# The second DFT stage and its inverse as 64x64 products on quarters of the array, with the exchanged rows from a second product

## The chip, the cores and the metric

The kernel runs on one core of a Trainium2 chip. A core has TensorE (PE, matrix products, with its weight loads listed as PEld), VectorE (DVE), ScalarE (ACT), GpSimd (POOL) and SyncE (SP, which here only issues transfers). Products go from SBUF to PSUM, which DVE and ACT empty. The metric is device time in microseconds, median of several runs; lower is better.

## The reference, cut to what matters

```python
def _A_ref(q, k, v, shift_k, ssm_k, ssm_D):      # B, S, D = 1, 2048, 640
    ...                                          # k_shift: 4-tap causal convolution of k
    kv = k_shift * v
    kv_f = rfft2(pad(kv, 2 * S), axes=(1, 2))    # per channel, length 4096
    kf_f = rfft2(pad(ssm_k, 2 * S))
    y = irfft2(kv_f * kf_f)[:, 0, :S, :] + kv * ssm_D
    return q * y

x = A_q
xn = layernorm(x)
s = _A_ref(xn, A_k, A_v, A_shift_k, A_ssm_k, A_ssm_D)
g = silu(gelu(xn @ w1 + b1) @ w2 + b2)           # F = 1728
return x + s * g
```

So there is a long convolution of kv with a filter for every channel, done by way of the frequency domain, and beside it a two-layer feed-forward network (FFN) over the same rows, whose output gates the convolution's.

## The kernel before, in words

**The convolution** is a DFT in two stages, written as matrix products in bf16. The filter and kv each go through the first stage (steps kf and uf, whole 128x128 weights WA and WB), are cast from PSUM to SBUF (ke, ue), stored to DRAM (ks, us: scrK, scrU) and loaded back in another order of rows (fl: kin; ml: uin). The second stage works on 32 groups g of 128 rows and 640 channels. Its weight matrix `mats[:, 0]` (F2m) holds four 32x32 blocks on the diagonal and zeros elsewhere; each block maps the rows of one small transform, with cosine and sine parts in alternating rows.

- `ff g` (k_f2, line 479): the filter's second stage, one call of mm2 (line 335), which makes two products, one for each half of 320 channels, into one "big" PSUM tile. `fe g` casts it into `Khat[:, g, :]`, on ACT or DVE.
- `mk g2` (swap_load, line 515): two copies by DMA on SP's queue, which put the rows of two groups of Khat into a ring buffer with each even row exchanged with the odd row beside it. The ring is the last 8 of Khat's 40 rows.
- `mu g` (u_f2, line 520): the second stage of kv, mm2 with the same weights, into one big tile.
- `mp g` (product, line 523): one DVE instruction of 1280 elements a partition. It multiplies the tile of mu with Khat and with the exchanged Khat, and so gives all four partial products of a complex multiplication as a pair tile p.
- `mc g` (inv1, line 530): the inverse of the second stage, for each half two accumulating products, with weights I1a on p's first part and I1b on its second, into one big tile. `me g` (line 537) casts it to SBUF on ACT or DVE, and `ms g2` (line 540) stores two groups to scrC on POOL's queue.

After that, `yl` loads scrC back, `y` makes the last inverse stage (whole weights GA, GB), and `yt`, `yo`, `ys` gate, add and store.

**The FFN** runs in four chunks of 512 rows. `h` (ffn1, line 373) is five products of 512 columns, `he` the GELU on ACT; `g` (ffn2, line 391) is 14 products of 320 columns, `ge` the SiLU on ACT and `gm` a multiplication on DVE. `tt` and `it` are transposes on PE, `te` and `ie` empty them.

**The order of all work is written by hand**: PLAN, lines 30 to 71, is a list of steps, and each engine works through its instructions in that order. Every engine's queue, that of PE too, is in order. Semaphores follow from tiles: an instruction that first writes a buffer waits for the last reader of the tile that held it before.

**PSUM** has 8 banks. `ps_ffn` has two tiles of one bank (h, g, tt). `ps_big` (line 108) has three tiles of two banks; ff, uf, kf, mu, mc, it, kt and y take them in turn, each from its first product to the cast or product that reads it. In the stage looked at here, PLAN runs for example `mu5 mp5 mk6 h31 he31 ml6 ff20 fe20.a mc3 me3.a ms1 ln15 mu6 mp6 mc4 me4.a mu7 mp7`: FFN steps fill PE between the convolution's.

Of the kernel before, what the change touches and what calls it, by code (L numbers as in the profile page):

```python
# [30 lines left out]
em K0 sp s A0 h0 h1 P2 ee.a A1 P1 P0 pt pb he0 he1 h2 he2 h3 he3 h4 he4 h5 he5 h6 he6 h7 he7 h8 he8 h9 he9 h10
he10 h11 he11 h12 he12 h13 he13 K3 ss cv8 cv0 B w cv1 cv2 cv3 cv4 cv5 cv6 cv9 cv10 cv11 cv12 cv13 cv14 K1 cv16
X1 ls4 ls5 ls7 ls6 lv1 C0 X3 cv17 cv18 g0 ge0 gm0 g1 ge1 gm1 ws0 cv19 g2 ge2 g3 ge3 g4 cv20 cv21 cv22 ws1 g5 lr1
ln7 ln5 ws2 C4 C3 C1 V0 cv7 cv15 C2 d kt0 kc0.a kt1 kc1.a kf0 kf1 ke0.a kt2 kc2.a V1 ln4 kf2 ke2.a cv24 cv23 X2
cv25 ke1.d ks0 gm2 ge4 ln6 kf3 ke3.d ks1 kf4 ke4.a gm4 ge5 kt3 kc3.d kf5 ke5.a ks2 V2 tt7 te7.a kt5 kc5.d tt9
te9.a kt4 gm5 kf7 cv26 cv27 cv28 kf6 kc4.a ke6.a ke7.a ks3 g6 ge6 kf8 ke8.a kf9 ke9.d ks4 kf10 ke10.a K2 tt8
te8.a kt6 kc6.d kf11 ke11.a ks5 kt9 kc9.d gm3 kf12 ke12.a tt5 te5.d tt6 te6.a uf1 kt7 kf13 kc7.a ke13.a ks6 g7
ge7 ls12 uf0 ue0.a ue1.d us0 cv29 cv30 cv31 V3 h14 he14 kf14 ke14.d kf15 ke15.d ks7 h15 he15 kt8 kc8.d kf19 kf18
ke18.a ke19.d ks9 kt10 kc10.a cv32 cv33 cv34 cv35 cv36 kf16 ke16.a kt12 cv40 kf17 kc12.a ke17.a ks8 h16 he16 uf3
uf2 ue2.a ue3.a us1 h17 he17 kf21 kf20 ke20.a ke21.d ks10 kt11 kc11.a h18 he18 uf5 uf4 ue4.a ue5.d us2 kf22  # L40
ke22.d ls10 h19 he19 kt14 kf24 ke24.d sm kf23 kc14.a ke23.a ks11 h20 he20 kf25 ke25.d ks12 kt13 kc13.d kf28
ke28.a h21 he21 uf6 ue6.a kf29 ke29.a ks14 uf7 ue7.a us3 h22 he22 h23 he23 kf26 ke26.a gm7 cv37 cv38 cv41 cv42
cv39 kf27 ke27.a ks13 kt15 kc15.d kf30 ke30.a kf31 ke31.a ks15 fl0 fl1 fl2 h24 he24 fl4 uf10 ue10.a gm6 ls15 ls8
ls9 uf8 ue8.a ls14 uf11 ue11.a us5 h25 he25 h26 he26 uf14 ue14.a cv43 ls13 lv3 lr3 h27 he27 cv44 ls11 lv2 lr2
cv45 cv46 cv47 uf12 ue12.a uf9 ue9.a us4 fl3 uf15 ue15.a us7 g8 ge8 gm8 ln13 ln9 uf13 ue13.a us6 fl5 g9 ge9 ff3
fe3.a ln12 ff1 fe1.d ln10 ff2 fe2.a cv56 ff0 fe0.a cv48 cv49 cv50 ln8 uf21 uf20 ue20.a ue21.a us10 ff8 fe8.a
ln11 g10 ge10 uf16 ue16.a ff6 fe6.d gm9 ff9 fe9.a fl7 ff5 fe5.a ff7 fe7.a fl9 ff4 fe4.a fl8 uf17 ue17.a us8 g11
ge11 cv51 cv52 cv53 cv54 cv55 ff11 fe11.a ff10 fe10.a fl6 uf18 ue18.d uf19 ue19.a us9 fl11 uf26 ue26.a cv57 cv58
cv59 uf24 ue24.a uf27 ue27.a us13 uf25 ue25.a us12 fl12 ff16 fe16.d ff17 fe17.a fl15 ff12 fe12.a tt12 te12.a
ff14 fe14.a cv60 cv61 cv62 cv63 ff18 fe18.a ff15 fe15.a fl13 g12 ff19 fe19.a fl10 uf22 ue22.d ff13 fe13.a fl14  # L50
uf31 gm11 ge12 uf30 ue30.a ue31.d us15 ff23 fe23.d gm12 uf23 ue23.a us11 gm10 tt14 te14.d uf29 uf28 ue28.d
ue29.a us14 mk0 ml0 ml1 mk1 mk2 mk3 ml2 ml3 ml5 ml4 ff31 fe31.a tt13 te13.a tt10 te10.d it0 ie0.d ff27 fe27.d
ff25 fe25.d g13 ge13 gm13 g14 ge14 gm14 ff29 fe29.d ln14 ff28 fe28.a ff24 fe24.d g15 ge15 gm15 ff21 fe21.a tt11
te11.d ff22 fe22.a mu0 mp0 ff26 fe26.a ml7 h28 he28 mu2 mp2 ml10 ml8 mu1 mp1 mk4 mc0 me0.a h29 he29 ff30 fe30.a
mu3 mp3 mk5 ml12 h30 he30 ml11 mc2 me2.a mu4 mp4 mc1 me1.a ms0 mu5 mp5 mk6 h31 he31 ml6 ff20 fe20.a mc3 me3.a
ms1 ln15 mu6 mp6 mc4 me4.a mu7 mp7 mk7 ml9 h32 he32 mu8 mp8 mc5 me5.a ms2 mc6 me6.a mu11 mp11 mc7 me7.a ms3 mu10
mp10 h33 he33 mu9 mp9 mk8 mk9 mc8 me8.a mc10 me10.a mu12 mp12 mu13 mp13 mk10 mc11 me11.a ms5 ml14 h34 he34 ml15
mc12 me12.a it1 ie1.d mc13 me13.a ms6 mu15 mp15 h35 he35 mu14 mp14 mk11 ml13 mc9 me9.a ms4 mu18 mp18 h36 he36
mc14 me14.a mu17 mp17 h37 he37 mu16 mp16 mk12 mc15 me15.a mu20 mp20 h38 he38 mu19 mp19 mk13 mc18 me18.a h39 he39
mu21 mp21 mk14 mc16 me16.a tt17 mc19 me19.a ms9 mc17 me17.a ms8 mu23 mp23 mc20 me20.a mu22 mp22 mk15 h40 he40  # L60
mc21 me21.a ms10 mu24 mp24 mu25 mp25 mc22 me22.a h41 he41 te17.d mc24 me24.a mu26 mp26 mc25 me25.a ms12 tt15
te15.a mu27 mp27 tt16 te16.d mc23 me23.a ms11 mc26 me26.a tt18 te18.d mu29 mp29 it3 ie3.a mu28 mp28 g16 ge16
gm16 mc27 me27.a ms13 it2 ie2.d tt19 te19.a mu31 mp31 mu30 mp30 ms7 q0 g17 ge17 gm17 mc28 me28.a mc31 mc29
me29.d ms14 mc30 me30.d me31.d ms15 yl5 yl2 yl0 yl4 yl3 yl1 yl6 yl11 yl15 q1 g18 ge18 gm18 g19 ge19 gm19 g20
ge20 gm20 g21 ge21 gm21 g22 ge22 gm22 g23 ge23 gm23 h42 he42 h43 he43 y0 yt0 yo0 h44 he44 h45 he45 h46 he46 y5
yt5 yl8 y4 yt4 yo4 yo5 ys2 y1 yt1 yo1 ys0 y3 yt3 h47 he47 h48 he48 h49 he49 h50 he50 h51 he51 y2 yt2 yl7 yl14
yl9 yl10 yl12 yo2 yo3 ys1 q2 h52 he52 h53 he53 h54 he54 h55 he55 y6 yt6 yl13 yo6 y7 yt7 yo7 ys3 q3 y8 yt8 yo8
y11 yt11 g24 ge24 g25 ge25 g26 y12 yt12 gm24 ge26 gm25 ga24 ga25 gs25 y15 yt15 g27 ge27 y14 yt14 y13 yt13 gm26
ga26 gm27 ga27 gs27 y9 yt9 yo9 ys4 y10 yt10 yo10 yo11 ys5 g28 ge28 gm28 ga28 g29 ge29 gm29 ga29 g30 ge30 gm30
ga30 gs30 g31 ge31 gm31 ga31 gs29 gs31  # L70
"""


# [1 line left out]
def kernel(  # L75
# [170 lines left out]
    sm = {}  # L246
# [49 lines left out]
                             bias=sin_bias[:])  # L296

    def small_mats():
        nc.vector.tensor_tensor(out=mats[:], in0=sm["sn"], in1=sm["mask"], op=ALU.mult)
# [35 lines left out]
    def mm2(ps, lhsT, rhs, start=True, stop=True):  # L335
        for h in range(2):
            nc.tensor.matmul(out=ps[:, h, 0:HALF], lhsT=lhsT, rhs=rhs[:, h * HALF:(h + 1) * HALF], start=start, stop=stop)  # L337
# [174 lines left out]
    def uin_load(g2):  # L512
        nc.sync.dma_start(out=take(("uin", g2), pools["line"], None, None, None), in_=pair_view(scrU)[g2])

    def swap_load(g2):
        ks = take(("ks", g2), pools["ring"], None, None, "ks")
        for a in range(2):
            nc.sync.dma_start(out=ks[a:P:2, :, :], in_=Khat[1 - a:P:2, 2 * g2:2 * g2 + 2, :])
# [4 lines left out]
    def product(g):
        p = pair_of(("p", g))
        swap = NG + g % NR
        nc.vector.tensor_tensor(out=p[:].rearrange("p k (h c) -> p k h c", h=2),  # L526
                                in0=live["mu", g][:, None, :, 0:HALF].to_broadcast([P, 2, 2, HALF]),
                                in1=Khat[:, g:swap + 1:swap - g, :].rearrange("p k (h c) -> p k h c", h=2), op=ALU.mult)

    def inv1(g):  # L530
        p, psC = live["p", g], big_of(("mc", g))
        for h in range(2):
# [1 line left out]
            nc.tensor.matmul(out=psC[:, h, 0:HALF], lhsT=I1a, rhs=p[:, 0, hs], start=True, stop=False)  # L534
            nc.tensor.matmul(out=psC[:, h, 0:HALF], lhsT=I1b, rhs=p[:, 1, hs], start=False, stop=True)  # L535
# [171 lines left out]
```

## Time and profile before

| what | value |
|---|---|
| median of 3 runs | 229.04 us (227.22 to 229.06) |
| span of the profiled execution, first to last instruction | 225.2 us |
| PE busy | 209.3 us |
| DVE busy | 183.2 us |
| ACT busy | 149.7 us |
| DMA: 50.7% by the hardware queue, 20.6% by POOL's | share of 16 engines' span |

The page gives the span of the profiled execution and not what lies around it; the median of the runs is 3.84 us above this span. A row of the groups reads: line, engine, operation, out<-in, shape, count, then busy time in us, mean ns of one, then idle time of the engine just before and who ended it. Products are pipelined: one is listed with some 0.3 us, from its start to its modelled end, while the next starts well before that. A row of the timeline has the start in us from the span's start, the length, and "xN" where N instructions in a row were put together.

### The profile page before, as it was taken

The page shows a single profiled execution, that of the slowest core. Times are in us where ns is not written, and L with a number is a line of the kernel's source. Part 1 is how long each engine was busy: PE and PEld are TensorE (multiplying, and loading weights), DVE is VectorE, ACT ScalarE, POOL GpSimd, SP SyncE. Part 2 cuts the span into 40 slices and gives each one's busy share as a digit, 9 for nine tenths or more (in the row PEclk, how much of TensorE's full clock was granted, in tenths as well). Part 3 has the DMA queues.
Part 4 walks back from the last instruction along what each step waited for, and adds up shares of the span by engine and source line. Part 5 has one row for each costly group of instructions (what it writes and reads, how often), then busy time and mean ns, then how long its engine had stood idle before and what let it go on. Part 6 is the DMA issues. An engine that isn't in the chain of part 4 may idle for free.

```text
span 225.2 us, 3912 instructions
## 1 busy us (share of the span) xinstructions
PE 209.3 (93%) x1420; PEld 131.5 (58%) x1420; DVE 183.2 (81%) x309; ACT 149.7 (66%) x232; POOL 42.5 (19%) x72
## 2 busy tenths in 40 slices
PE   7869989899999899979999988999999999999993
PEld 4624457677555556645765544565777755457771
DVE  7799999989989999999859998999996125445792
ACT  3946697998988999999549665576762263671111
POOL 8000011032232345030200221203222000100010
...
GB/s 215 347 381 357 406 410 277 218 193 198 303 186 189 178 209 388 185 320 324 320 167 286 335 399 361 273 231 254 273 118 140 215 367 153 119 260 388 80 92 116
DMA packets 25209, 57.61 MB, mean 256 GB/s; under 512 B 2854, under 2 KB 14055, under 8 KB 25190
## 3 DMA queue, kind: packets, MB, share of 16 engines
q1 hardware_dynamic: 20726, 39.66, 50.7%
q0 software_dynamic: 4320, 17.70, 20.6%
...
## 4 chain that ended last, share of the span: by engine, by line
PE 59%; issue 13%; ACT 11%; DVE 7%; DMA 7%; SPq 1%; POOL 1%; DVEq 0%; POOLq 0%; ACTq 0%
PE g L396 20%; PE h L377 20%; ACT Khat L135 5%; DMA prm<-in_B_b_dram 4%; PE uf L337 3%; PE mc L534 2%; DMA scrC<-c 2%; PE mc L535 2%; PE kf L337 2%; PE mu L337 2%; PE y L553 2%; PE y L554 2%; DVE p L526 2%; DVE Khat L136 2%; PE ff L337 1%
## 5 line engine op out<-in xcount | busy, mean ns | idle before, releaser
L377 PE MATMUL h<-xnT,w_sb 128*128 128x512 bf16 x280 | 65.8, 379 | 1.3 <-ACT hT L383 1.0
L396 PE MATMUL g<-w_sb,hT 128*128 128x320 bf16 x448 | 63.7, 299 | 0.6 <-ACT sl L401 0.6
L396 PEld LDWEIGHTS <-hT 128*128 128x128 bf16 x448 | 43.8, 98 | 18.1 <-issue 0.8
L383 ACT ACTIVATE hT<-h,b_f 128x512 bf16<-128x512 f32 (+1 forms) x56 | 38.3, 690 | 23.2 <-PE h L377 20.7
L526 DVE TENSOR_TENSOR p<-mu,Khat 128x1280 bf16<-128x1280 f32 x32 | 45.8, 1484 | 3.1 <-PE mu L337 2.1
L377 PEld LDWEIGHTS <-w_sb 128*128 128x128 bf16 x280 | 27.3, 98 | 29.3 <-issue 1.5
L401 ACT ACTIVATE sl<-g 128x320 bf16<-128x320 f32 x32 | 14.0, 439 | 36.1 <-PE g L396 32.5
L135 ACT CAST c<-mc 128x640 bf16<-128x640 f32 x29 | 19.9, 692 | 6.5 <-PE mc L535 5.7
L541 POOL DMA_DIRECT2D scrC<-c x16 | 11.5, 718 | 51.9 <-ACT c L135 47.7
L406 DVE TENSOR_TENSOR xn<-xn,sl 128x320 bf16<-128x320 bf16 x32 | 10.0, 320 | 13.7 <-ACT sl L401 13.5
L469 DVE TENSOR_TENSOR uc<-uc,kvtmp 128x1280 bf16<-128x1280 bf16 x24 | 19.8, 824 | 0.7
L473 DVE TENSOR_TENSOR kvtmp<-kh,w_exp 128x1280 bf16<-128x1280 bf16 x24 | 19.7, 819 | 0.5
L534 PE MATMUL mc<-p,mats 128*128 128x320 bf16 x64 | 18.1, 298 | 1.6 <-DVE p L526 1.1
L560 DVE TENSOR_TENSOR t<-y,xn 128x640 bf16<-128x640 f32 x12 | 9.8, 820 | 10.6 <-PE y L554 10.5
L337 PEld LDWEIGHTS <-mats 128*128 128x128 bf16 x128 | 12.0, 97 | 10.8 <-issue 3.8
L535 PE MATMUL mc<-p,mats 128*128 128x320 bf16 x64 | 18.1, 298 | 0.0
L135 ACT CAST Khat<-uf 128x640 bf16<-128x640 f32 x26 | 17.0, 697 | 0.4 <-PE uf L337 0.4
L135 ACT CAST Khat<-ff 128x640 bf16<-128x640 f32 x24 | 15.5, 699 | 0.5 <-PE ff L337 0.4
L135 ACT CAST Khat<-kf 128x640 bf16<-128x640 f32 x22 | 15.1, 711 | 0.3 <-PE kf L337 0.2
L437 POOL DMA_DIRECT2D scrK<-Khat x16 | 8.9, 554 | 29.7 <-ACT Khat L135 16.6
L337 PE MATMUL mu<-kh,mats 128*128 128x320 bf16 x64 | 13.6, 298 | 0.8 <-DMA kh<-scrU 0.4
L337 PE MATMUL ff<-kin,mats 128*128 128x320 bf16 x64 | 12.3, 298 | 1.3 <-ACT Khat L135 1.3
...
## 6 DMA issues: line engine op xcount, KB each, us to landing
...
```

The costliest lines, as they stand in the source:

```text
L135: return nc.scalar.copy(out=out_ap, in_=in_ap)
L337: nc.tensor.matmul(out=ps[:, h, 0:HALF], lhsT=lhsT, rhs=rhs[:, h * HALF:(h + 1) * HALF], start=start, stop=stop)
L377: nc.tensor.matmul(out=ps[:, :], lhsT=w1_sb[:, t, ft * P:(ft + 1) * P], rhs=xnT[:, t, :], start=(t == 0), stop=(t == DT - 1))
L383: nc.scalar.activation(out=hT[0:M, ft, :], in_=live["h", i][0:M, :], func=ACT.Gelu_apprx_tanh, bias=b1_f[0:M, ft:ft + 1], scale=1.0)
L396: nc.tensor.matmul(out=ps[:, 0:HALF], lhsT=hT[0:M, ft, q * P:(q + 1) * P], rhs=w2_sb[0:M, ft, hs], start=(ft == 0), stop=(ft == FT - 1))
L401: nc.scalar.activation(out=sl[:], in_=live["g", i][:, 0:HALF], func=ACT.Silu)
L469: nc.vector.tensor_tensor(out=uc[:], in0=uc[:], in1=kvtmp[:], op=ALU.add)
L473: nc.vector.tensor_tensor(out=(kvtmp if s else uc)[:], in0=kh[:, r0:r0 + KC, :], in1=w_exp[:, j:j + 1, :].to_broadcast([P, KC, D]), op=ALU ...
L526: nc.vector.tensor_tensor(out=p[:].rearrange("p k (h c) -> p k h c", h=2), in0=live["mu", g][:, None, :, 0:HALF].to_broadcast([P, 2, 2, HA ...
L534: nc.tensor.matmul(out=psC[:, h, 0:HALF], lhsT=I1a, rhs=p[:, 0, hs], start=True, stop=False)
L535: nc.tensor.matmul(out=psC[:, h, 0:HALF], lhsT=I1b, rhs=p[:, 1, hs], start=False, stop=True)
L541: nc.gpsimd.dma_start(out=pair_view(scrC)[g2], in_=live["c", g2][:])
```

## The change

It does four things and leaves the rest of the program as it is.

1. `ff`: each of the two products becomes two of 64x64 weights, from the two diagonal blocks of F2. For one half of the channels the blocks' outputs go to the same half of the partitions as the inputs, for the other half of the channels to the opposite one, so that the four products of a group use the four quarters of the array.
2. `mu`: the same, and a second set with F2X, a copy of F2 with neighbouring columns exchanged, which gives the result with exchanged rows. Each half of the channels gets a big PSUM tile of its own: bank 0 the plain result, bank 1 the exchanged one. A mu thus has eight products and two big tiles.
3. `mp`: one instruction for each half (mp 2g and mp 2g+1), which multiplies both banks of the half's tile with Khat. The step `mk` is gone, and with it its 32 copies.
4. `mc`: four quarter products for I1A and four for I1B, accumulated, which put the partitions back in order.

`small_mats` makes the matrix F2X with two DVE copies. In PLAN the 16 `mk` steps are left out and each `mp g` is replaced in place by `mp 2g, mp 2g+1`; nothing else in the order changes.

```diff
-    mats = consts.tile([P, 3, P], BF16, name="mats")
-    F2m, I1a, I1b = (mats[:, i, :] for i in range(3))
+    mats = consts.tile([P, 4, P], BF16, name="mats")
+    F2, I1A, I1B, F2X = range(4)
+    QB = 64
...
     def small_mats():
-        nc.vector.tensor_tensor(out=mats[:], in0=sm["sn"], in1=sm["mask"], op=ALU.mult)
+        nc.vector.tensor_tensor(out=mats[:, 0:3, :], in0=sm["sn"], in1=sm["mask"], op=ALU.mult)
+        for c in range(2):
+            nc.vector.tensor_copy(out=mats[:, F2X, c::2], in_=mats[:, F2, 1 - c::2])
...
+    def blocks(out, m, rhs, turn, start=True, stop=True):
+        for i in range(P // QB):
+            j = (i + turn) % (P // QB)
+            a, b = (slice(x * QB, (x + 1) * QB) for x in ((i, j) if m in (F2, F2X) else (j, i)))
+            nc.tensor.matmul(out=out[b, :], lhsT=mats[a, m, a], rhs=rhs[a, :], start=start, stop=stop)
+
+    def half(h):
+        return slice(h * HALF, (h + 1) * HALF)
...
     def k_f2(g):
-        mm2(big_of(("ff", g)), F2m, live["kin", g // 2][:, g % 2, :])
+        ps = big_of(("ff", g))
+        for h in range(2):
+            blocks(ps[:, h, 0:HALF], F2, live["kin", g // 2][:, g % 2, half(h)], 2 * g + h)
...
-    def swap_load(g2):
-        ks = take(("ks", g2), pools["ring"], None, None, "ks")
-        for a in range(2):
-            nc.sync.dma_start(out=ks[a:P:2, :, :], in_=Khat[1 - a:P:2, 2 * g2:2 * g2 + 2, :])
-
     def u_f2(g):
-        mm2(big_of(("mu", g)), F2m, live["uin", g // 2][:, g % 2, :])
-
-    def product(g):
+        ps = [big_of(("mu", 2 * g + h)) for h in range(2)]
+        for x, m in enumerate((F2, F2X)):
+            for h in range(2):
+                blocks(ps[h][:, x, 0:HALF], m, live["uin", g // 2][:, g % 2, half(h)], 2 * g + h)
+
+    def product(i):
+        g, h = divmod(i, 2)
         p = pair_of(("p", g))
-        swap = NG + g % NR
-        nc.vector.tensor_tensor(out=p[:].rearrange("p k (h c) -> p k h c", h=2),
-                                in0=live["mu", g][:, None, :, 0:HALF].to_broadcast([P, 2, 2, HALF]),
-                                in1=Khat[:, g:swap + 1:swap - g, :].rearrange("p k (h c) -> p k h c", h=2), op=ALU.mult)
+        nc.vector.tensor_tensor(out=p[:, :, half(h)], in0=live["mu", i][:, :, 0:HALF],
+                                in1=Khat[:, g:g + 1, half(h)].to_broadcast([P, 2, HALF]), op=ALU.mult)
 
     def inv1(g):
         p, psC = live["p", g], big_of(("mc", g))
-        for h in range(2):
-            hs = slice(h * HALF, (h + 1) * HALF)
-            nc.tensor.matmul(out=psC[:, h, 0:HALF], lhsT=I1a, rhs=p[:, 0, hs], start=True, stop=False)
-            nc.tensor.matmul(out=psC[:, h, 0:HALF], lhsT=I1b, rhs=p[:, 1, hs], start=False, stop=True)
+        for x, m in enumerate((I1A, I1B)):
+            for h in range(2):
+                blocks(psC[:, h, 0:HALF], m, p[:, x, half(h)], 2 * g + h, x == 0, x == 1)
```

More of the change, by code (lines that the diff above doesn't have):

```diff
@@ L30 @@
 PLAN = """
[L31 to L70, printed above, removed]
+em K0 sp s A0 h0 h1 P2 ee.a A1 P1 P0 pt pb he0 he1 h2 he2 h3 he3 h4 he4 h5 he5 h6 he6 h7 he7 h8 he8 h9 he9 h10 he10
@@ new lines @@
+h11 he11 h12 he12 h13 he13 K3 ss cv8 cv0 B w cv1 cv2 cv3 cv4 cv5 cv6 cv9 cv10 cv11 cv12 cv13 cv14 K1 cv16 X1 ls4 ls5
+ls7 ls6 lv1 C0 X3 cv17 cv18 g0 ge0 gm0 g1 ge1 gm1 ws0 cv19 g2 ge2 g3 ge3 g4 cv20 cv21 cv22 ws1 g5 lr1 ln7 ln5 ws2 C4
+C3 C1 V0 cv7 cv15 C2 d kt0 kc0.a kt1 kc1.a kf0 kf1 ke0.a kt2 kc2.a V1 ln4 kf2 ke2.a cv24 cv23 X2 cv25 ke1.d ks0 gm2
+ge4 ln6 kf3 ke3.d ks1 kf4 ke4.a gm4 ge5 kt3 kc3.d kf5 ke5.a ks2 V2 tt7 te7.a kt5 kc5.d tt9 te9.a kt4 gm5 kf7 cv26 cv27
+cv28 kf6 kc4.a ke6.a ke7.a ks3 g6 ge6 kf8 ke8.a kf9 ke9.d ks4 kf10 ke10.a K2 tt8 te8.a kt6 kc6.d kf11 ke11.a ks5 kt9
@@ new lines @@
+kc9.d gm3 kf12 ke12.a tt5 te5.d tt6 te6.a uf1 kt7 kf13 kc7.a ke13.a ks6 g7 ge7 ls12 uf0 ue0.a ue1.d us0 cv29 cv30 cv31
+V3 h14 he14 kf14 ke14.d kf15 ke15.d ks7 h15 he15 kt8 kc8.d kf19 kf18 ke18.a ke19.d ks9 kt10 kc10.a cv32 cv33 cv34 cv35
+cv36 kf16 ke16.a kt12 cv40 kf17 kc12.a ke17.a ks8 h16 he16 uf3 uf2 ue2.a ue3.a us1 h17 he17 kf21 kf20 ke20.a ke21.d
+ks10 kt11 kc11.a h18 he18 uf5 uf4 ue4.a ue5.d us2 kf22 ke22.d ls10 h19 he19 kt14 kf24 ke24.d sm kf23 kc14.a ke23.a
+ks11 h20 he20 kf25 ke25.d ks12 kt13 kc13.d kf28 ke28.a h21 he21 uf6 ue6.a kf29 ke29.a ks14 uf7 ue7.a us3 h22 he22 h23
@@ new lines @@
+he23 kf26 ke26.a gm7 cv37 cv38 cv41 cv42 cv39 kf27 ke27.a ks13 kt15 kc15.d kf30 ke30.a kf31 ke31.a ks15 fl0 fl1 fl2
+h24 he24 fl4 uf10 ue10.a gm6 ls15 ls8 ls9 uf8 ue8.a ls14 uf11 ue11.a us5 h25 he25 h26 he26 uf14 ue14.a cv43 ls13 lv3
+lr3 h27 he27 cv44 ls11 lv2 lr2 cv45 cv46 cv47 uf12 ue12.a uf9 ue9.a us4 fl3 uf15 ue15.a us7 g8 ge8 gm8 ln13 ln9 uf13
+ue13.a us6 fl5 g9 ge9 ff3 fe3.a ln12 ff1 fe1.d ln10 ff2 fe2.a cv56 ff0 fe0.a cv48 cv49 cv50 ln8 uf21 uf20 ue20.a
+ue21.a us10 ff8 fe8.a ln11 g10 ge10 uf16 ue16.a ff6 fe6.d gm9 ff9 fe9.a fl7 ff5 fe5.a ff7 fe7.a fl9 ff4 fe4.a fl8 uf17
@@ new lines @@
+ue17.a us8 g11 ge11 cv51 cv52 cv53 cv54 cv55 ff11 fe11.a ff10 fe10.a fl6 uf18 ue18.d uf19 ue19.a us9 fl11 uf26 ue26.a
+cv57 cv58 cv59 uf24 ue24.a uf27 ue27.a us13 uf25 ue25.a us12 fl12 ff16 fe16.d ff17 fe17.a fl15 ff12 fe12.a tt12 te12.a
+ff14 fe14.a cv60 cv61 cv62 cv63 ff18 fe18.a ff15 fe15.a fl13 g12 ff19 fe19.a fl10 uf22 ue22.d ff13 fe13.a fl14 uf31
+gm11 ge12 uf30 ue30.a ue31.d us15 ff23 fe23.d gm12 uf23 ue23.a us11 gm10 tt14 te14.d uf29 uf28 ue28.d ue29.a us14 ml0
+ml1 ml2 ml3 ml5 ml4 ff31 fe31.a tt13 te13.a tt10 te10.d it0 ie0.d ff27 fe27.d ff25 fe25.d g13 ge13 gm13 g14 ge14 gm14
@@ new lines @@
+ff29 fe29.d ln14 ff28 fe28.a ff24 fe24.d g15 ge15 gm15 ff21 fe21.a tt11 te11.d ff22 fe22.a mu0 mp0 mp1 ff26 fe26.a ml7
+h28 he28 mu2 mp4 mp5 ml10 ml8 mu1 mp2 mp3 mc0 me0.a h29 he29 ff30 fe30.a mu3 mp6 mp7 ml12 h30 he30 ml11 mc2 me2.a mu4
+mp8 mp9 mc1 me1.a ms0 mu5 mp10 mp11 h31 he31 ml6 ff20 fe20.a mc3 me3.a ms1 ln15 mu6 mp12 mp13 mc4 me4.a mu7 mp14 mp15
+ml9 h32 he32 mu8 mp16 mp17 mc5 me5.a ms2 mc6 me6.a mu11 mp22 mp23 mc7 me7.a ms3 mu10 mp20 mp21 h33 he33 mu9 mp18 mp19
+mc8 me8.a mc10 me10.a mu12 mp24 mp25 mu13 mp26 mp27 mc11 me11.a ms5 ml14 h34 he34 ml15 mc12 me12.a it1 ie1.d mc13
@@ new lines @@
+me13.a ms6 mu15 mp30 mp31 h35 he35 mu14 mp28 mp29 ml13 mc9 me9.a ms4 mu18 mp36 mp37 h36 he36 mc14 me14.a mu17 mp34
+mp35 h37 he37 mu16 mp32 mp33 mc15 me15.a mu20 mp40 mp41 h38 he38 mu19 mp38 mp39 mc18 me18.a h39 he39 mu21 mp42 mp43
+mc16 me16.a tt17 mc19 me19.a ms9 mc17 me17.a ms8 mu23 mp46 mp47 mc20 me20.a mu22 mp44 mp45 h40 he40 mc21 me21.a ms10
+mu24 mp48 mp49 mu25 mp50 mp51 mc22 me22.a h41 he41 te17.d mc24 me24.a mu26 mp52 mp53 mc25 me25.a ms12 tt15 te15.a mu27
+mp54 mp55 tt16 te16.d mc23 me23.a ms11 mc26 me26.a tt18 te18.d mu29 mp58 mp59 it3 ie3.a mu28 mp56 mp57 g16 ge16 gm16
@@ new lines @@
+mc27 me27.a ms13 it2 ie2.d tt19 te19.a mu31 mp62 mp63 mu30 mp60 mp61 ms7 q0 g17 ge17 gm17 mc28 me28.a mc31 mc29 me29.d
+ms14 mc30 me30.d me31.d ms15 yl5 yl2 yl0 yl4 yl3 yl1 yl6 yl11 yl15 q1 g18 ge18 gm18 g19 ge19 gm19 g20 ge20 gm20 g21
+ge21 gm21 g22 ge22 gm22 g23 ge23 gm23 h42 he42 h43 he43 y0 yt0 yo0 h44 he44 h45 he45 h46 he46 y5 yt5 yl8 y4 yt4 yo4
+yo5 ys2 y1 yt1 yo1 ys0 y3 yt3 h47 he47 h48 he48 h49 he49 h50 he50 h51 he51 y2 yt2 yl7 yl14 yl9 yl10 yl12 yo2 yo3 ys1
+q2 h52 he52 h53 he53 h54 he54 h55 he55 y6 yt6 yl13 yo6 y7 yt7 yo7 ys3 q3 y8 yt8 yo8 y11 yt11 g24 ge24 g25 ge25 g26 y12
@@ L71 @@
+yt12 gm24 ge26 gm25 ga24 ga25 gs25 y15 yt15 g27 ge27 y14 yt14 y13 yt13 gm26 ga26 gm27 ga27 gs27 y9 yt9 yo9 ys4 y10
+yt10 yo10 yo11 ys5 g28 ge28 gm28 ga28 g29 ge29 gm29 ga29 g30 ge30 gm30 ga30 gs30 g31 ge31 gm31 ga31 gs29 gs31
 """
@@ L668 @@
         "fl": kin_load, "ff": k_f2, "fe": k_f2_out, "it": i2_tr, "ie": i2_out,
-        "ml": uin_load, "mk": swap_load, "mu": u_f2, "mp": product, "mc": inv1, "me": inv1_out, "ms": c_store,
+        "ml": uin_load, "mu": u_f2, "mp": product, "mc": inv1, "me": inv1_out, "ms": c_store,
         "q": xq_load, "yl": cab_load, "y": inv2, "yt": gate, "yo": out_add, "ys": out_store,
```

## The prediction

> **What bounds the kernel now.** I read the page first, then busy time by stretches, the groups of instructions, the waits, and at last the order of time inside the stage that the change rebuilds.
>
> ```profile
> span 225.2 us, 3912 instructions
> PE 209.3 (93%) x1420; PEld 131.5 (58%) x1420; DVE 183.2 (81%) x309; ACT 149.7 (66%) x232; POOL 42.5 (19%) x72
> ...
> PE   7869989899999899979999988999999999999993
> ...
> DVE  7799999989989999999859998999996125445792
> ```
>
> TensorE (PE) looks like the bound at 93%, but that is a mean over stages. The second row of digits shows VectorE (DVE) as full as PE up to about slice 30, then far below. The tile view dates the rebuilt stage, that of the steps mu, mp and mc:
>
> ```profile
> L337 PE MATMUL mu<-kh,mats x64: 296/299/309, 117.5 to 166.5; 128*128 128x320 bf16 x64
> L526 DVE TENSOR_TENSOR p<-mu,Khat x32: 1477/1481/1492, 118.0 to 168.1; 128x1280 bf16<-128x1280 f32 x32
> ```
>
> Busy time in that stage, and in the one of the ff and uf steps ahead of it (columns: PE, PEld, DVE, ACT, POOL; then clock and DMA share):
>
> ```profile
> 117.50:171.00 53.50, 51.14 (x342) 31.38 (x343) 49.67 (x43) 36.88 (x55) 10.04 (x14) 1.00 0.79 278
> ```
> ```profile
> 86.50:117.50 31.00, 28.32 (x206) 18.60 (x204) 27.42 (x47) 23.68 (x42) 5.18 (x10) 1.00 0.80 274
> ```
>
> So in the rebuilt stage two engines are near the bound together: PE 51.1 and DVE 49.7 of 53.5 us. Relief on PE alone leaves DVE's floor; anything added to DVE lengthens the stage almost at once. The groups say what DVE does there, and give the durations for the rest:
>
> ```profile
> L526 DVE TENSOR_TENSOR p<-mu,Khat 128x1280 bf16<-128x1280 f32 x32 | 45.8, 1484 | 3.1 <-PE mu L337 2.1 <-DMA Khat<-Khat 0.8
> ...
> L534 PE MATMUL mc<-p,mats 128*128 128x320 bf16 x64 | 18.1, 298 | 1.6 <-DVE p L526 1.1 <-ACT c L135 0.2
> ...
> L337 PE MATMUL ff<-kin,mats 128*128 128x320 bf16 x64 | 12.3, 298 | 1.3 <-ACT Khat L135 1.3
> ...
> L560 DVE TENSOR_TENSOR t<-y,xn 128x640 bf16<-128x640 f32 x12 | 9.8, 820 | 10.6 <-PE y L554 10.5
> ```
>
> The products take 45.8 us; all other DVE work of the stage is 49.67 - 45.8 = 3.9 us. DVE is idle for only 3.1 us ahead of products. In order of time the present rhythm is:
>
> ```profile
> 110.22 1.54 DVE L136 CAST Khat<-ff 128x640 bf16<-128x640 f32 x2
> ```
> ```profile
> 137.50 2.89 DVE L526 TENSOR_TENSOR p<-mu,Khat 128x1280 bf16<-128x1280 f32 x2 [0.93 <-PE mu L337]
> ...
> 139.33 0.30 PE L534 MATMUL mc<-p,mats 128*128 128x320 bf16 x1
> ...
> 139.46 0.30 PE L535 MATMUL mc<-p,mats 128*128 128x320 bf16 x1
> ...
> 139.60 0.61 PE L488 MATMUL it<-ident,WA 128*128 128x128 bf16 x8
> ...
> 140.44 0.30 PE L534 MATMUL mc<-p,mats 128*128 128x320 bf16 x1 [0.23 <-DVE p L526]
> ...
> 140.98 0.43 PE L337 MATMUL mu<-kh,mats 128*128 128x320 bf16 x2
> ...
> 141.51 5.68 DVE L526 TENSOR_TENSOR p<-mu,Khat 128x1280 bf16<-128x1280 f32 x4 [0.53 <-PE mu L337]
> ```
>
> Four products run on without a pause (5.68 us, one per (5.68 - 1.48)/3 = 1.40 us), because a mu takes one of the three "big" PSUM tiles and the next mu is finished before the product ahead of it ends. That run-ahead is what the change touches. Two latencies are here too. From DVE's end to a waiting PE: 137.50 + 2.89 = 140.39 to 140.44, 0.05 us. From a last matmul's start to the product: the two mu matmuls start 0.135 apart (as 139.33 and 139.46 do), the second at 141.115; the product starts at 141.51, 0.395 later.
>
> **The change, part by part.** *Unit price of a quarter product* (64x64 weights, 320 columns). No row shows one. Ends: four at once, 0.135/4 = 0.034 us each; one after another, 0.135 us each. The nearest row is the smallest product here, 64 columns behind a weight load each:
>
> ```profile
> 10.48 0.60 PEld L305 LDWEIGHTS <-skp 128*128 128x128 bf16 x10
> ```
> ```profile
> 10.53 0.72 PE L305 MATMUL psw<-ident,skp 128*128 128x64 bf16 x10
> ```
> ```profile
> L305 PE MATMUL psw<-ident,skp x40: 219/348/348, 3.9 to 11.0; 128*128 128x64 bf16 x40
> ```
>
> Ten loads with their products go at (0.72 - 0.22)/9 = 0.055 us a pair, and transposes of twice the columns at (0.61 - 0.22)/7 = 0.056. That looks like the price of issuing a load and a product. A quarter product is issued the same way and four share the streaming, so I take s = 0.055 us and keep 0.034 and 0.135 as ends.
>
> *ff:* two products of 0.135 become four of s: 0.27 to 0.22 us, 29 of them ahead of the stage, 1.5 us less PE (ends -3.9 and +7.8). The end of that stage is not set by PE:
>
> ```profile
> 109.77 0.54 POOL L447 DMA_DIRECT2D scrU<-Khat  x1 [0.74 <-ACT Khat L135]
> ...
> 114.53 0.88 SPq L513 DMA_DIRECT2D kh<-scrU  x2
> ```
>
> The last store of U leaves at 109.77, the first load of it can be issued at 114.53, and the first mu runs at 117.5: this round trip covers the ff steps behind it. Taken: -0.5 us.
>
> *mc:* four products of 0.135 (0.54 us) become eight of s (0.44). PE only.
>
> *mu:* two products (0.27 us) become eight of s (0.44).
>
> PE in the stage afterwards: 14 h, 2 g and 44 transposes stay, by the chain's pieces
>
> ```profile
> 141.42 1.08 PE h L377 x5
> ...
> 163.16 1.90 PE g L396 x14
> ```
>
> 14 x 1.08 + 2 x 1.90 + 44 x 0.056 = 21.4 us; quarters 32 x 16 + 3 ff x 4 = 524 x 0.055 = 28.8; together 50.2 (ends 39.2 and 92.1) against 48.1 now by the same count. No relief at my price.
>
> *mp:* one product instruction of 1.40 to 1.48 us becomes two of half the size. L560 has their shape: 0.82 us alone, and two such conversions back to back take 1.54 (the row of 110.22, start to start 0.72). So 1.54 per pair, 32 x 1.54 = 49.3 us against 45.8: **+3.5 us** (ends +0.3, if pairs also chain at 0.72, and +6.7 at 0.82 each). DVE's floor becomes 49.3 + 3.9 = 53.2 us, the whole present stage.
>
> *The new wait.* A mu now takes two of the three big tiles, for its two halves. With one mc (or ff, it) between two mu, that one takes the third tile, and the next mu's tiles are those that the products of the mu before are still reading. Its second matmul pair (the other half) waits until the last product has ended, and DVE then has no finished tile. Per such place: 0.05 (DVE to PE) + 3s from the second pair's first quarter to the last of the first half's exchanged pair + 0.395 = 0.61 us. With two steps between, even the first tile is the one read last: 0.05 + 5s + 0.395 = 0.72. With three or four, a step ahead of mu waits in the same way: 0.05 + 13s + 0.395 = 1.16 and, with an it and an mc, 1.67. I counted the plan: of 31 passages from mu to mu, 9 have no such step between (no stall: a tile is free), 13 have one, 7 two, one three, one four. 13 x 0.61 + 7 x 0.72 + 1.16 + 1.67 = 15.8 us. At s = 0.034 it is 13.8, at 0.067 (two quarters at a time) 16.9. Behind the waiting matmul PE's whole queue stands (mc, h), so ACT's casts and POOL's stores of C come later too. The 3.9 us of other DVE work lies partly in these pauses; I credit half: **+15.8 - 1.9 = +13.9 us**.
>
> *mk removed:* 32 copies leave SP's queue.
>
> ```profile
> L518 SPq DMA_DIRECT2D Khat<-Khat x32: 464/588/1441, 106.5 to 156.7; - x32
> ```
> ```profile
> DVE p L526 <- PE mu L337: 2.1, 4, 0.9
> ...
> DVE p L526 <- DMA Khat<-Khat: 0.8, 3, 0.3
> ...
> PE mu L337 <- DMA kh<-scrU: 0.4, 1, 0.4
> ```
>
> 32 x 0.588 = 18.8 us of SP time, from which the loads of U behind them gain. What the stage can get back is bounded by DVE's waits of 2.1 + 0.8 us; the 53.5 us hold 3.8 us of DVE idleness. I take the 0.8 and the pause of 0.93 as gone, 1.7, and the other 2.1 as staying.
>
> *small_mats:* two more DVE copies of 64 columns, on the chain where the row stands:
>
> ```profile
> 69.32 0.47 DVE mats L299
> ```
>
> That instruction writes 384 columns; two of 64 cost less than it together, and more than nothing. Taken: +0.2.
>
> **Sum.** Stage: 49.3 products + 3.9 other + 13.9 stalls + 2.1 idle = 69.2 us, against 53.5: +15.7. With -0.5 and +0.2: **+15.4**. What follows the stage keeps its order and its cover, so it only shifts. The profiled span becomes 225.2 + 15.4 = 240.6; the runs' median of 229.04 lies 3.84 above that span, so I predict 244.4 us.
>
> **The rivals.**
>
> *PE's relief decides (faster).* If quarters run four at once, PE saves 48.1 - 39.2 = 8.9 us in the stage and 3.9 ahead of it. For: PE is the fuller engine and carries most of the chain. Against: DVE's floor of 53.2. If the stalls cost nothing the stage stays at 53.2 less 1.7, and with about 2.5 of the ff relief the time is near 225. It decides only if a passage stalls for less than about (1.7 + 2.5)/22 = 0.2 us, and the 0.395 us behind a last matmul alone is twice that.
>
> *Quarters do not overlap (the change does not do what it says).* Then s = 0.135: PE needs 92.1 us in the stage, +38.6, and up to 7.8 more ahead of it, of which I take 5: about 273 us. Against: no row speaks for it except that none shows an overlap. In pairs, s = 0.067, the sum is about 246 and still my forecast.
>
> *Emptying the array between whole and quarter products.* A matmul ends 0.298 after it starts, and the next starts after 0.135; if each change of form lets the array run empty, it costs 0.16 us. The plan has 24 runs of quarter steps in the stage and 14 ahead: 48 x 0.16 = 7.7 and 28 x 0.16 = 4.5 us of PE. In the stage PE would need 57.9 of 69.2 us, so only passages with an h in them grow, about 12 by 0.2; of the 4.5 I let 2 show: 244.4 + 4.4 = 249 us. The Trainium skill, page TensorEngine Tiling (Array Packing), section Tiling Modes (Key Properties), says that a change of tiling mode drains TensorE; no run here shows it, as all products of this kernel but a single small one use the whole array.
>
> **How the numbers follow.** My forecast (stalls on the two PSUM tiles): 0.72. Its low end takes every term at its cheap end: +0.3 for mp, 13.8 - 3.9 for stalls with all other DVE work inside them, -1.7, and -1.5 for ff, +7.0 or 236. Its high end: 6.7 + 16.9 + 0.2 = +23.8 or 253. Emptying on top, 249: 0.12. Serial quarters, 273: 0.08. PE's relief, 225: 0.08. That range holds the first two and leaves out the last two, 0.16 together, and a tail of the first. A measurement of this kernel tells about 1% (2.3 us) from no change: faster 0.06 (most of the last rival), same 0.03, slower 0.91.
>
> **What would show it.** Right: the stage from first mu to last mc near 69 us; DVE idle ahead of products for 13 to 18 us with PE mu as the releaser, in 20 or so pauses of 0.5 to 0.9 us; PE mu waiting for DVE p; products of 0.82 us, 64 of them; span behind the stage unchanged. Wrong: pauses under 0.2 us (then the relief rival); PE busy with starts 0.135 apart inside mu and mc (serial); a gap of 0.16 at each first quarter behind an h (emptying); or the ff stage moving by more than 3 us.

## The result, and the profile after

The changed kernel takes 243.75 us (median, 241.62 to 244.82) against 228.13 us of the kernel before; ratio 1.0687, 95% interval 1.0603 to 1.0771. Predicted were 244.4 us. Medians here and below are over all runs of a kernel, while a ratio leaves out runs over 1.5% above that kernel's fastest. The profiled execution took 241.62 us with a span of 239.8.

The page of the changed kernel, span, busy time and the slices of PE and DVE:

```profile
span 239.8 us, 4641 instructions
## 1 busy us (share of the span) xinstructions
PE 211.7 (88%) x1788; PEld 122.9 (51%) x1804; DVE 187.2 (78%) x343; ACT 149.8 (62%) x232; POOL 42.3 (18%) x72
...
PE   7869989899998988789976779897888999999993
...
DVE  7799999989899999997776886987778312626692
```

From slice 19 to about slice 30 both rows now read mostly 6 to 8, where they read mostly 8 or 9 before: the two engines take turns. The tile view dates the stage; the first row of stretches below is that stage, the second the one ahead of it (columns as in the prediction):

```profile
L344 PE MATMUL mu<-kh,mats x256: 292/296/320, 117.3 to 181.4; 64*64 64x320 bf16 x128
L536 DVE TENSOR_TENSOR p<-mu,Khat x64: 814/816/826, 118.1 to 182.6; 128x640 bf16<-128x640 f32 x64
```
```profile
117.30:185.40 68.10, 55.18 (x663) 25.35 (x665) 53.74 (x75) 37.12 (x55) 10.01 (x14) 1.00 0.45 145
```
```profile
86.50:117.30 30.80, 27.15 (x266) 16.04 (x265) 27.47 (x47) 23.63 (x42) 5.28 (x10) 1.00 0.81 274
```

The stage from the first mu to the last mc grew from 53.4 to 68.1 us, +14.7. The stage begins at 117.3 us as it began at 117.5, and 54.4 us follow it, as 54.3 did. All of the loss lies in this stage: DVE works 53.7 us in it (49.6 before) and is idle for 14.4 us (3.8 before). The groups, and who waited for whom inside the stage:

```profile
L536 DVE TENSOR_TENSOR p<-mu,Khat 128x640 bf16<-128x640 f32 x64 | 49.4, 819 | 10.9 <-PE mu L344 8.2 <-issue 0.8 <-ACT xnT L133 0.8
...
L344 PE MATMUL mu<-kh,mats 64*64 64x320 bf16 x256 | 20.7, 306 | 7.5 <-DVE p L536 3.9 <-ACT c L133 2.3 <-ACT Khat L133 0.7
...
L344 PEld LDWEIGHTS <-mats 64*64 64x64 bf16 x640 | 18.0, 104 | 37.6 <-issue 34.5 <-DMA kin<-scrK 0.5
```
```profile
DVE p L536 <- PE mu L344: 8.2, 15, 1.1
PE mu L344 <- DVE p L536: 3.9, 10, 0.8
PE mu L344 <- ACT c L133: 2.3, 7, 0.6
```

Product waits for mu and mu waits for product: a circle that in the kernel before was nearly absent (2.1 and 0.2 us). One turn of it, between mu4 and mu5 with the step mc1 between, in order of time on DVE, on PE and on ACT:

```profile
126.04 1.55 DVE L536 TENSOR_TENSOR p<-mu,Khat 128x640 bf16<-128x640 f32 x2 [0.43 <-PE mu L344]
128.19 1.55 DVE L536 TENSOR_TENSOR p<-mu,Khat 128x640 bf16<-128x640 f32 x2 [0.60 <-PE mu L344]
```
```profile
126.56 0.47 PE L344 MATMUL mc<-p,mats 64*64 64x320 bf16 x8 [0.44 <-ACT c L133]
126.92 0.32 PE L344 MATMUL mu<-kh,mats 64*64 64x320 bf16 x2
127.81 0.46 PE L344 MATMUL mu<-kh,mats 64*64 64x320 bf16 x6 [0.58 <-ACT c L133]
128.21 1.04 PE L387 MATMUL h<-xnT,w_sb 128*128 128x512 bf16 x4
```
```profile
127.07 0.69 ACT L133 CAST c<-mc 128x640 bf16<-128x640 f32 x1 [0.56 <-PE mc L344]
```

The first pair of the new mu runs as soon as the first of the two products has ended (126.04 + 0.82 = 126.86, to 126.92). Of the other six, four need the second tile and two stand behind those in PE's queue; they start at 127.81, when both products are done (127.59) and DVE is idle. The next product starts at 128.19, after 0.60 us; h, which had nothing to wait for, stands behind them in PE's queue. In this turn it was ACT's cast of mc1, done at 127.76, that gave the second tile back, not the product done at 127.59. The text ahead of the prediction says that steps take the big tiles in turn; here they do not do so strictly.

### The profile page after: what moved, and what is told of

Its sections match the earlier page's. It is cut to its first block, busy times and chain, and to the rows that moved or that the text cites. A ratio compares the mean times of both kernels' runs of the same rounds, so it can differ in the third digit from the quotient of the medians.

```text
span 239.8 us, 4641 instructions
## 1 busy us (share of the span) xinstructions
PE 211.7 (88%) x1788; PEld 122.9 (51%) x1804; DVE 187.2 (78%) x343; ACT 149.8 (62%) x232; POOL 42.3 (18%) x72
## 5 line engine op out<-in xcount | busy, mean ns | idle before, releaser
L387 PE MATMUL h<-xnT,w_sb 128*128 128x512 bf16 x264 | 63.4, 379 | 2.9 <-issue 1.1
L536 DVE TENSOR_TENSOR p<-mu,Khat 128x640 bf16<-128x640 f32 x64 | 49.4, 819 | 10.9 <-PE mu L344 8.2
L406 PEld LDWEIGHTS <-hT 128*128 128x128 bf16 x448 | 43.2, 98 | 19.1 <-issue 2.1
L387 PEld LDWEIGHTS <-w_sb 128*128 128x128 bf16 x280 | 26.2, 98 | 31.7 <-issue 4.9
L411 ACT ACTIVATE sl<-g 128x320 bf16<-128x320 f32 x32 | 13.9, 439 | 38.4 <-PE g L406 34.7
L344 PEld LDWEIGHTS <-mats 64*64 64x64 bf16 x640 | 18.0, 104 | 37.6 <-issue 34.5
L344 PE MATMUL mu<-kh,mats 64*64 64x320 bf16 x256 | 20.7, 306 | 7.5 <-DVE p L536 3.9
L344 PE MATMUL mc<-p,mats 64*64 64x320 bf16 x256 | 14.3, 304 | 4.2 <-DVE p L536 2.1
L447 POOL DMA_DIRECT2D scrK<-Khat x16 | 8.8, 552 | 29.8 <-ACT Khat L133 16.6
L457 POOL DMA_DIRECT2D scrU<-Khat x16 | 8.9, 553 | 23.9 <-ACT Khat L133 23.8
L344 PE MATMUL ff<-kin,mats 64*64 64x320 bf16 x128 | 8.8, 311 | 2.3 <-ACT Khat L133 2.0
```

Of the source, the lines that this page charges most:

```text
L344: nc.tensor.matmul(out=out[b, :], lhsT=mats[a, m, a], rhs=rhs[a, :], start=start, stop=stop)
L387: nc.tensor.matmul(out=ps[:, :], lhsT=w1_sb[:, t, ft * P:(ft + 1) * P], rhs=xnT[:, t, :], start=(t == 0), stop=(t == DT - 1))
L406: nc.tensor.matmul(out=ps[:, 0:HALF], lhsT=hT[0:M, ft, q * P:(q + 1) * P], rhs=w2_sb[0:M, ft, hs], start=(ft == 0), stop=(ft == FT - 1))
L411: nc.scalar.activation(out=sl[:], in_=live["g", i][:, 0:HALF], func=ACT.Silu)
L536: nc.vector.tensor_tensor(out=p[:, :, half(h)], in0=live["mu", i][:, :, 0:HALF], in1=Khat[:, g:g + 1, half(h)].to_broadcast([P, 2, HALF]), ...
```

## The experiments

Two theories. **A**: a mu now holds two of the three big PSUM tiles, so PE and DVE can no longer run ahead of each other. **B**: the loss comes from the quarters themselves (eight products, changes between whole and quarter products) or from the product's split on DVE. Where totals are unclear, the length of the stage is compared, since dips of the granted clock ahead of it came with starts between 117.3 and 121.8 us from run to run; e8_two_tiles_first had the longest, in its first 30 us (the number behind POOL's busy time is the clock, 0.89; from 15.9 to 22.7 us it is 0.50):

```profile
0.00:30.00 30.00, 23.96 (x128) 11.62 (x131) 25.41 (x65) 15.70 (x24) 5.45 (x15) 0.89 0.97 340
```

**e7_two_tiles: two tiles alone.** From the kernel before, with the products split as in e4_split_product below, each half reading its own tile:

```diff
 def u_f2(g):
-    mm2(big_of(("mu", g)), F2m, live["uin", g // 2][:, g % 2, :])
+    ps = [big_of(("mu", 2 * g + h)) for h in range(2)]
+    for h in (1, 0):
+        nc.tensor.matmul(out=ps[h][:, 0, 0:HALF], lhsT=F2m, rhs=live["uin", g // 2][:, g % 2, h * HALF:(h + 1) * HALF], start=True, stop=True)
```

> The kernel before with split products (as in e4_split_product), and the two halves of each mu in two big PSUM tiles in place of one; the product for the second half's tile is issued first, so that the first half too is done only when the second tile was free. No quarter, no exchanged product: copies by DMA and the work of every engine are those of e4_split_product. Theory (two tiles of three take away the run-ahead): a pause of 0.05 + 0.135 + 0.395 = 0.58 us at the 22 passages with a step between, 12.8 us, less what other DVE work hides: 228.5 + 10 to 14 = 238 to 243. Rival (the pauses come from eight quarter products, their changes of form, or the exchanged product): as e4_split_product, 227 to 231.

Measured: 242.96 us, ratio 1.0645 (1.0566 to 1.0724), inside the range and nearly the whole loss, with PE's products, the copies and DVE's work as in e4_split_product. The stage of the one and of the other:

```profile
118.20:187.40 69.20, 55.59 (x339) 31.41 (x343) 53.42 (x75) 37.40 (x55) 10.01 (x14) 1.00 0.62 210
```
```profile
117.50:172.30 54.80, 51.44 (x344) 30.98 (x342) 51.64 (x75) 36.97 (x55) 10.01 (x14) 1.00 0.77 267
```

The second is e4_split_product. Two tiles for one, with the first half behind the second, make 14.4 us. This shows A and leaves little for B.

**e4_split_product: the split alone.**

```diff
-        nc.vector.tensor_tensor(out=p[:].rearrange("p k (h c) -> p k h c", h=2),
-                                in0=live["mu", g][:, None, :, 0:HALF].to_broadcast([P, 2, 2, HALF]),
-                                in1=Khat[:, g:swap + 1:swap - g, :].rearrange("p k (h c) -> p k h c", h=2), op=ALU.mult)
+        for h in range(2):
+            hs = slice(h * HALF, (h + 1) * HALF)
+            nc.vector.tensor_tensor(out=p[:, :, hs], in0=live["mu", g][:, h:h + 1, 0:HALF].to_broadcast([P, 2, HALF]),
+                                    in1=Khat[:, g:swap + 1:swap - g, hs], op=ALU.mult)
```

> The kernel before, with each product as two instructions of 640 elements out of the one PSUM tile; whole products on PE, copies as before. Theory: only DVE's extra work of 49.4 - 45.8 = 3.6 us is added, in a stage where DVE is idle for 3.8: ratio 1.00 to 1.018, 228 to 232.5. Rival (the split on DVE is most of the loss): 236 or more.

Measured: 228.5 us, ratio 1.0062 (1.0018 to 1.0106). The products take

```profile
L528 DVE TENSOR_TENSOR p<-mu,Khat 128x640 bf16<-128x640 f32 x64 | 47.7, 816 | 2.3 <-PE mu L337 1.0
```

47.7 us where they run on (45.8 whole), and the stage is 1.4 us longer. Of the changed kernel's 49.4 us, 1.9 is the split; the other 1.7 I put down mostly to pauses that break the chain, since the same split takes 48.9 in e7_two_tiles.

**e3_quarters_only: quarters alone.** The kernel before with `blocks` in k_f2, u_f2 (into one tile) and inv1, copies and whole product instructions kept:

```diff
-        mm2(big_of(("mu", g)), F2m, live["uin", g // 2][:, g % 2, :])
+        ps = big_of(("mu", g))
+        for h in range(2):
+            blocks(ps[:, h, 0:HALF], F2, live["uin", g // 2][:, g % 2, half(h)], 2 * g + h)
```

> The kernel before, with quarter products in ff, mu and mc alone: one PSUM tile a mu, one product instruction of 1280 elements, exchanged rows by DMA copies as before. Theory: no new pauses; DVE's work of the stage (45.8 + 3.9 us) stays the floor, PE gets 3.9 to 13 us of relief less 76 changes of form at 0.09 (6.9 us): 225 to 229, ratio to before 0.985 to 1.005. Rival (quarters or their changes of form are the loss): 234 or more.

Measured: 227.94 us, ratio 0.9971 (0.9920 to 1.0021), no difference that this can tell. The stage:

```profile
119.00:171.50 52.50, 44.71 (x543) 21.97 (x540) 49.35 (x43) 36.03 (x55) 10.00 (x14) 1.00 0.80 281
```

PE is busy for 44.7 us in place of 51.0, DVE as before, and the stage is 0.9 us shorter. The quarters do relieve PE, and in the median this is worth almost nothing. It may be worth more at an equal clock. Of the runs with a mean granted clock of 0.988 to 0.993, the five of e3_quarters_only took 227.0 us in the mean and the six of the kernel before beside them 229.2; but only 1 of its 10 runs had a clock of 0.996 or more, against 12 of 19. Whether the lower clock comes from the idle time on PE was not tested.

**e2_whole_array: the changed kernel without quarters.** `blocks` makes one whole product, `nc.tensor.matmul(out=out, lhsT=mats[:, m, :], rhs=rhs, ...)`.

> The changed kernel with whole 128x128 products in ff, mu and mc (weights F2, F2X, I1A, I1B whole), two PSUM tiles a mu and split products as they are. No change of form is left on PE; a mu is four products (0.54 us), a mc four. Theory: the pauses stay, each longer by some 0.15 us because a mu needs 0.135 for each product (22 x 0.15 = 3.3), and PE has 0.25 us more in each mu and mc, most of it inside DVE's pauses: 245 to 252. Rival (changes of form cause the loss, 0.09 to 0.16 us each, 76 of them): faster than the changed kernel by 5 to 10 us, 234 to 239.

Measured: 247.46 us, ratio 1.0866 (1.0784 to 1.0948), inside the range. With no change of form left it is slower than the changed kernel, and DVE is idle for 19.1 us of the stage in place of 14.4. Rival B's first half falls: inside this change the quarters earn some 4 us, as the theory has it because what PE does in the circle is shorter.

**e1_half_outer and e8_two_tiles_first: the first half no longer behind the second.** In the changed kernel's u_f2 the loops were exchanged, in e7_two_tiles' the order of the halves:

```diff
-        for x, m in enumerate((F2, F2X)):
-            for h in range(2):
+        for h in range(2):
+            for x, m in enumerate((F2, F2X)):
```
```diff
-    for h in (1, 0):
+    for h in (0, 1):
```

> The changed kernel, with the loops of mu exchanged: first the four products of the first half (F2, F2X), then the four of the second. The first half no longer waits for the second half's tile. Theory (pauses come from the two PSUM tiles of a mu): where one step lies between two mu, 13 passages, the pause of about 0.49 us goes, since the first half's tile is free one product earlier; where two or more lie between, it stays. 13 x 0.49 = 6.4 us less than the changed kernel's 243.75: 237.5, between 235 and 240; DVE idle ahead of products from 10.9 to about 5. Rival (pauses are PE's lateness after changes between whole and quarter products, or the split of the product on DVE alone): neither is touched, 242 to 246.

> As e7_two_tiles, but the first half's product is issued first, so it waits only for its own tile. Theory: where one short step (mc) lies between two mu the pause goes; where an h lies between, PE, held at the second half until the product ends, starts its h late and a pause stays. Some 2 to 6 us less than e7_two_tiles: 234 to 239. Rival (order inside a mu does not matter): the same as e7_two_tiles within 1 us.

Measured: 240.67 us, ratio 1.0580 (1.0496 to 1.0663), and 242.13 us, ratio 1.0579 (1.0475 to 1.0682). The stages fall from 68.1 to 66.1 us and from 69.2 to 65.2:

```profile
119.70:185.80 66.10, 56.68 (x671) 26.60 (x665) 53.45 (x75) 37.16 (x55) 10.01 (x14) 1.00 0.46 149
```
```profile
121.80:187.00 65.20, 54.43 (x338) 31.41 (x342) 53.12 (x75) 37.36 (x55) 10.03 (x14) 1.00 0.66 224
```

Both totals miss their ranges. For e1_half_outer the gain is a third to a half of what I expected, and DVE's idle time ahead of products fell from 10.9 to 8.7 us, not to 5. For e8_two_tiles_first the stage came down by 4.0 us as expected and the total did not: in the profiled execution the stage began 3.6 us later than in e7_two_tiles, behind the dip of the clock shown above, and three of its four runs have a mean clock of 0.992 or less, where none of e7_two_tiles' has. By the stages, the order counts. Read passage by passage, pauses went where a lone mc lies between two mu (mu5 0.60 to none, mu7 0.29 to 0.04, mu10 0.33 to none). Where an h lies there they stayed or grew at nine of 14 passages (mu24 0.43 to 0.94, mu9 0.09 to 0.76) and shrank by 0.07 to 0.38 at five: PE stands at the second half until the product ahead has ended, starts its 1.08 us of h only then, and is late for the next mu. So A has a second part, which the prediction mentioned as what stands behind the waiting matmul but gave no price.

**e11_spread.** e1_half_outer with mc steps put off, so that of 31 passages only 3 hold two steps that take a big tile (9 before); PLAN alone is edited, for example `mu8 mp16 mp17 mc5 me5.a ms2 mu11 mp22 mp23 mc6 me6.a mu10`.

> e1_half_outer with mc steps put off so that nearly every passage from mu to mu holds at most one step that takes a big PSUM tile. Theory (where two or more lie between, the next mu's first tile is the one that is read last): the pauses at those passages, 4.1 + 0.6 + 1.4 us in e1_half_outer, shrink to some 2 to 3; stage from 66.1 to 61 to 64 us, total 236 to 239. Rival (they are PE's lateness, as steps are only moved): stage and total as in e1_half_outer, 65 to 67 and 239.5 to 242.

Measured: 243.64 us, ratio 1.0677 (1.0614 to 1.0740), a miss. The pauses did go where I said (mu11, mu12, mu23 to none), but the steps put off now lie beside an h, where five passages stand at 0.9 to 1.2 us, and one product waits for 3.0 us on an mc that was put off too long:

```profile
DVE p L536 <- PE mc L344: 3.6, 2, 3.0
```

DVE's idle time in the stage rose from 12.6 to 16.6 us, and the stage from 66.1 to 69.3. With so few tiles, moving steps moved the pauses.

**e5_quarters_act and e6_before_act: DVE's floor.** Five casts of the stage moved from DVE to ACT in place (`te17.d` to `te17.a`, likewise te16, te18, ie1, ie2), in e3_quarters_only and in the kernel before.

> e3_quarters_only (one tile, whole product instructions, quarters on PE) with five casts of the stage (te16, te17, te18, ie1, ie2) moved in place from DVE to ACT. They are 3 x 0.42 + 2 x 0.69 = 2.6 us of DVE. Theory (DVE is the floor of that stage once PE has relief): 2 to 3 us less than e3_quarters_only: 225 to 226, ratio 0.985 to 0.992. Rival (PE's order of steps or ACT is as tight): no gain, 227 to 229.

> The kernel before with the same five casts moved from DVE to ACT, whole products. Theory (PE, 51.1 of 53.5 us busy, is the next bound there): at most 1.5 us less, 226.5 to 228, and 1 us or more above e5_quarters_act. Rival (DVE alone bounds the stage): as much gain as e5_quarters_act has, 225 to 226.

Measured: 228.96 us, ratio 1.0050 (1.0003 to 1.0097), and 229.53 us, ratio 1.0049 (0.9999 to 1.0098). In e5_quarters_act the rival's time came out, and e6_before_act lies above what either expected: 2.6 us of DVE work less brought nothing; DVE's idle time in the stage rose from 3.1 to 6.2 us and from 3.8 to 6.5. Why was not settled. In e6_before_act the waits of products for mu grew, from 2.1 to 4.6 us. In e5_quarters_act a single wait for a copy is the largest piece of it:

```profile
DVE p L540 <- DMA Khat<-Khat: 2.0, 1, 2.0
```

Right behind that wait, from 135.5 to 138.9 us, the granted clock is 0.50, inside the stage, and eight of the ten runs have a mean clock of 0.985. So e5_quarters_act is not a clean test of DVE's floor.

**e9_quarters_shift and e10_before_shift: filling PE's freed time.** In e3_quarters_only and in the kernel before, h40, h41, g16 and g17 earlier and g18, g19 inside the stage, for example

```diff
-mu29 mp29 it3 ie3.a mu28 mp28 g16 ge16 gm16 mc27 me27.a
+mu29 mp29 g17 ge17 gm17 it3 ie3.a mu28 mp28 g18 ge18 gm18 mc27 me27.a
```

> e3_quarters_only (one tile a mu, copies by DMA, quarters on PE) with PE's freed time filled: h40 and h41 a passage earlier, and two g steps more (g18, g19; g16 and g17 earlier) inside the stage, 3.8 us of PE work that now stands behind it, where PE is never idle. Theory (the quarters' relief on PE, 5.4 us more idle time than before, was real and only lay idle): the stage grows by less than what is moved into it: 1 to 3 us less than the kernel before, ratio 0.985 to 0.996. Rival (the idle time lies in pieces that whole g steps cannot use): the stage grows by the 3.8 us, ratio 0.997 to 1.005.

> The kernel before with the same steps moved and nothing else (whole products). Theory (PE has no free time there: 51.1 of 53.5 us busy): the stage grows by what is moved in or more, ratio 1.00 to 1.01, and at least 1 us above e9_quarters_shift. Rival (only the order mattered): the same as e9_quarters_shift.

Measured: 228.99 us, ratio 1.0019 (0.9980 to 1.0058), and 231.84 us, ratio 1.0136 (1.0080 to 1.0192). So with the same order the quarters are worth some 2.7 us by the ratios, but against the kernel before nothing is won: e9_quarters_shift missed its range, with the rival's time, and the ratio of e10_before_shift lies above its range. The stage of e9_quarters_shift grew from 52.5 to 58.4 us, and that of e10_before_shift from 53.4 to 59.8, both by more than the 3.8 us moved in; in the first the granted clock is 0.51 from 133.5 to 136.9 us, so its growth is not clean. No version here is shown to be faster than the kernel before.

## Why the prediction was right, point by point

- **Where the loss lies: right.** Stage 69.2 us predicted, 68.1 measured; what is ahead of it and behind it is unchanged to 0.2 us.
- **mp, +3.5 us: right in size** (49.4 against 45.8, +3.6), though e4_split_product shows that the split alone is +1.9; the rest goes mostly with the pauses.
- **Pauses and idle time of DVE, 13.9 + 2.1 = 16.0 us: 14.4 measured.** That the two tiles are the cause is shown by e7_two_tiles. The sign given for it was too strong: DVE is idle ahead of products for 10.9 us, not 13 to 18, and for 8.2 of them in 15 waits with mu as the releaser, not some 20. By number of steps between two mu, DVE's idle time between the last product of the one and the first of the next, other DVE work taken off (the predicted prices are before the credit of 1.9 us for such work):

| steps between | passages | predicted, us each | measured mean, us |
|---|---|---|---|
| 0 | 9 | 0 | 0.06 |
| 1 | 13 | 0.61 | 0.41 |
| 2 | 7 | 0.72 | 0.66 |
| 3 | 1 | 1.16 | 0.95 |
| 4 | 1 | 1.67 | 1.66 |

The passages add up to 13.1 us, against the 13.9 predicted.

- **Who gives the second tile back: partly wrong.** The step said that with one step between, both tiles are those that the products are still reading. Of the waits of mu in the stage 10 ended with a product and 7 with ACT's cast of the mc between, as in the turn shown. There the pause is set by mc, its cast of 0.69 us and the second half: 0.60 us at mu5, 0.30 at mu7.
- **The price of such a pause, 0.61 us: too high.** From the second pair's start to the product it counted three quarter products, 0.165 us, and 0.395 behind them. In the turn shown the whole is 128.19 - 127.81 = 0.38 us, as the quarters start together. So where a product gives the tile back and one step lies between, the pause is 0.43 to 0.49 us (mu4, mu17, mu24, mu28).
- **PE's lateness: named, not priced.** At mu2, mu3, mu21 and mu26, 2.5 us together, mu itself waits for no tile: PE comes late to it, behind an h. At mu26 PE had stood 0.27 us at the mc ahead of that h:

```profile
167.89 0.47 PE L344 MATMUL mc<-p,mats 64*64 64x320 bf16 x8 [0.27 <-DVE p L536]
168.29 1.25 PE L387 MATMUL h<-xnT,w_sb 128*128 128x512 bf16 x5
169.47 0.47 PE L344 MATMUL mc<-p,mats 64*64 64x320 bf16 x8
169.77 0.44 PE L344 MATMUL mu<-kh,mats 64*64 64x320 bf16 x8
```
```profile
170.25 0.82 DVE L536 TENSOR_TENSOR p<-mu,Khat 128x640 bf16<-128x640 f32 x1 [0.61 <-PE mu L344]
```

The count of steps gave these four pauses nearly the right size, 2.7 us, by a wait that they do not have. That part of the agreement is luck.
- **Price of a quarter product, 0.055 us: too high.** mc's eight in the last rows run from 169.47 to 169.77 with no wait behind them, 0.30 us, 0.038 each, near the cheap end of 0.034. Four start within some 0.01 us of each other: one is listed with up to 0.32 us, and four of an mc take 0.33 together.

```profile
143.91 0.33 PE L344 MATMUL mc<-p,mats 64*64 64x320 bf16 x4 [0.27 <-DVE p L536]
```

In PE's own busy time the price decided nothing, since PE has time to spare: idle 12.9 us in the stage by the gaps of its products.
- **mk, small_mats, ff: right that they are small.** The stage's start moved by 0.2 us. DVE's wait for copies is gone.
- **Rivals.** PE's relief: the relief is real (e3_quarters_only) and bought nothing that the median shows. Serial quarters: no. A change of form does cost time, less than I priced: the last of the four h listed at 144.53 starts at 144.53 + 1.03 - 0.38 = 145.18, and the mc behind it at 145.49, 0.31 later where products of h follow each other after 0.215:

```profile
144.53 1.03 PE L387 MATMUL h<-xnT,w_sb 128*128 128x512 bf16 x4 [0.16 <-issue]
145.49 0.47 PE L344 MATMUL mc<-p,mats 64*64 64x320 bf16 x8
```

0.09 us where 0.16 was allowed. The Trainium skill, page TensorEngine Tiling (Array Packing), section Tiling Modes (Key Properties), states that such a change drains TensorE. The trace shows the 0.09 us, but not whether the array runs empty: the last h is listed until 145.18 + 0.38 = 145.56, after the mc starts, and these ends are modelled. The cost lies in PE's idle time and is outweighed by the quarters (e2_whole_array).
- **"DVE's floor is the whole present stage": only half true.** Adding to DVE lengthens the stage (e4_split_product, +1.4 us), but taking 2.6 us away did not shorten it (e6_before_act; e5_quarters_act has the dip of the clock inside its stage).
- **From span to runs.** I put 3.84 us between span and median; in the profiled execution it was 241.62 - 239.8 = 1.8, as in every other run on record (1.7 to 1.8). The 3.84 set the median beside the span of a faster execution; the other 2.0 us are spread between executions. With 1.8 the sum would have given 242.4, and that the total came within 1 us owes something to this.
